# First four quads of a block attention with MLP: fused mask and maximum, value sums off TensorE, one transfer per quad, and a new order

## The chip, the cores and the metric

One core of one Trainium2 chip runs the whole kernel. The metric is the device time of the program in microseconds (us); of each kernel the median of several runs is taken. A profile of one execution gives, beside it, the time of every instruction on the core's engines: TensorE (PE, with its weight loads PEld), VectorE (DVE), ScalarE (ACT), GpSimd (POOL), and SyncE (SP), which here issues nearly all transfers. "Span" is the time from the first to the last instruction of that execution. KB are 1,024 bytes.

## The reference

Attention of 4 sequences of 768 tokens, 8 heads of 64, in which a token sees the tokens within 15 places, and beside them 24 summaries of its whole sequence: one per block of 32 tokens, the maximum of the keys and the mean of the values. Its result goes through an MLP.

```python
k_sum = k.reshape(B, H, nb, block, D).max(axis=3)       # block = 32, nb = 24
v_sum = v.reshape(B, H, nb, block, D).mean(axis=3)
scores_l = scale * np.matmul(q, k.transpose(0, 1, 3, 2))
scores_s = scale * np.einsum('bhsd,bhnd->bhsn', q, k_sum) + np.log(block)
scores_l_m = np.where(abs(pos[:, None] - pos[None, :]) < 16, scores_l, -1e9)
a = softmax(np.concatenate([scores_l_m, scores_s], axis=-1))
attn = np.matmul(a, np.concatenate([v, v_sum], axis=2))
...
h = x @ w_in                                            # (3072, 512) @ (512, 2048)
g = h * erf(softplus(h))
out = g @ w_out                                         # (3072, 2048) @ (2048, 512)
```

## The kernel before

The 3,072 tokens are six chunks of 512, the 8 heads four pairs; a chunk and a pair make a **quad**, of which there are 24. A quad has eight blocks of 64 queries, each against a window of 96 keys and 24 summaries: 120 columns (`NK`, with `LW` = 96). The MLP runs in 24 periods, four per chunk, each for 512 of the 2,048 inner columns: `mm1` makes h (line L836), `hout`, `soft`, `erfs` and `gsplit` make g, `mm2` adds g times w_out into four output banks (L1006 and L1010; from the ninth period on h is made from seven products instead, L879, L882 and L888). Quads are made ahead of the period that needs them.

The first four quads open the program, and nothing of the MLP can run before them. For each quad p:

- `load_qk_first` brings its keys (384 KB, L510) and queries (256 KB, L511); `load_vw_first` brings its windows of values (512 KB, L518). The values as such, from which the means come, are two transfers of 768 KB for all four quads (`load_v_first`, L515), tokens on partitions.
- `ksum_first` takes the 24 block maxima of the keys on VectorE (L521).
- `scores`: TensorE writes a mask into two PSUM banks (`mask`: per bank a bf16 matmul of an identity with `mask_h`, L588, and one that adds log 32, L589), then adds the products of queries with keys and with the summaries (L597).
- `softmax`: VectorE takes the maximum of each block (`red`: two reductions, L636, and a scaling, L638); ScalarE takes the exponential from PSUM with its sum (L644); VectorE makes reciprocals (L648, L649) and normalises (L654), or ScalarE does (L657).
- `vsum_first`: six matmuls with a selecting matrix `pick` (L527) add the values of 32 tokens each, for all four quads in one bank; ScalarE copies the bank (L531), and for each quad its 24 rows are repeated into the window tile `vwf`: on ScalarE three times and by a DMA once (L535).
- `transp` (L684, copied by ScalarE, L689), `av` (the product with the values, L729) and `xsplit` (high part of x on ScalarE, low part on VectorE, L748) give the input of `mm1`.

The weights come as sixteen raw tiles of 1 MB (`load_w`, L334), the first two w_in tiles first. `convert` makes a float32 tile of each on VectorE (L354, L357, L360, about 128x1024 elements each), and `split` a high part on ScalarE and a low part on VectorE (L376). A matmul of h needs both parts of x and both of w. From quad 4 on masks are not made on TensorE: `add` is one VectorE instruction for each block (L630) that adds the mask to the scores, writes the result, and gives the negative maximum; `MQ` = 4 is the quad from which this holds.

The order of all work is made when the program is built: `Plan` records each step with its engines, a cost for each, and what it reads and writes; `order` walks through time by these costs, takes on each engine the ready step with the smallest key, and lets a step that may run on two engines go to the one that ends first. `TUNE` shifts keys, and pins some steps to an engine. While TensorE has a gap in that plan, `busy` puts in matmuls on zeros (L1058) that write a bank named `idle`, until the first step that needs that bank. Each engine then executes its list in order, waiting at each instruction for what it needs. SP's transfers take eight semaphores in turn, so that a transfer is issued only when the eighth before it has landed.

## Time and profile before

| what | before |
|---|---|
| time, median of 3 runs | 600.77 us (600.4 to 601.37) |
| span of the profiled execution | 599.2 us |
| TensorE busy | 591.9 us, 99% of the span |
| VectorE busy | 476.3 us, 79% |
| ScalarE busy | 425.4 us, 71% |
| GpSimd busy | 4.0 us, 1% |
| read from and written to memory | 135.66 and 31.46 MB |

Busy time is the union of an engine's instructions. Matmuls overlap each other, and a busy TensorE may be at filler work. An engine's busy share says little by itself where stages differ, so the rows below are read by stretches of time: the opening up to the first matmul of h, and the rest. The chain of waits is followed from the last instruction back to what released each step; one that starts with SP's issue and a transfer means that the transfer queue was the limit there.

### The profile page before, as it was taken

How to read it: one execution, taken by the hardware profiler on the slowest of the kernel's cores; microseconds unless marked ns; L12 is line 12 of the kernel's file. 1: busy time of each engine (PE TensorE's matmuls, PEld its weight loads, DVE VectorE, ACT ScalarE, POOL GpSimd, SP SyncE). 2: the span in 40 equal slices, each digit the busy share in tenths (PEclk: the TensorE clock that was granted, in tenths of full speed). 3: DMA queues.
4: the chain of work that ended last, by engine and by line, in shares of the span. 5: the costliest groups of instructions: out<-in, count | busy, mean ns of one | idle time of the engine just before them, and what ended most of it. 6: DMA issues, size and time to landing. Idle time of an engine off the chain costs nothing.

```text
span 599.2 us, 11732 instructions
## 1 busy us (share of the span) xinstructions
PE 591.9 (99%) x4515; PEld 486.9 (81%) x4515; DVE 476.3 (79%) x1001; ACT 425.4 (71%) x827; POOL 4.0 (1%) x30
## 2 busy tenths in 40 slices
PE   8999999999999999999999999999999999999997
PEld 4675666878888889889888888888888888888885
DVE  5999999888999987867989769669778677656552
ACT  6989889989979894674886964746646654852571
POOL 2000000000000000000000000000000000000000
PEclk9999999999999999999999999999999999999999
DMA  8999768578987989899898889777798863764622
GB/s 313 350 412 357 288 232 308 205 258 293 314 349 244 363 310 336 307 357 363 311 366 315 321 315 326 284 278 284 261 320 275 298 236 141 259 236 175 244 71 71
DMA packets 47955, 169.94 MB, mean 284 GB/s; under 512 B 4444, under 2 KB 17692, under 8 KB 35356
## 3 DMA queue, kind: packets, MB, share of 16 engines
q1 hardware_dynamic: 47324, 168.67, 77.7%
q8 instruction: 35, 0.57, 0.4%
q10 hardware_dynamic: 576, 0.52, 0.3%
q14 instruction: 20, 0.16, 0.1%
HBM read 135.66 MB, written 31.46 MB: 279 GB/s over the span
## 4 chain that ended last, share of the span: by engine, by line
PE 95%; DMA 2%; DVE 1%; SPq 1%; issue 0%; ACT 0%; DVEq 0%
PE ops L1010 41%; PE h L836 15%; PE ha L888 11%; PE hb L882 7%; PE ops L1006 5%; PE hb L888 4%; PE hb L879 4%; PE pA L597 3%; PE px L732 3%; DMA rw<-w_in 2%; PE px L729 1%; PE pA L684 1%; PE pB L597 0%; SPq L515 0%; SPq L511 0%; SPq L510 0%
## 5 line engine op out<-in xcount | busy, mean ns | idle before, releaser
L1010 PE MATMUL ops<-w,gh 128*128 128x512 f32 x704 | 230.2, 393 | 0.0
L1010 PEld LDWEIGHTS ops<-w,gh 128*128 128x128 f32 x704 | 132.3, 188 | 27.7 <-issue 0.9
L1010 PE MATMUL ops<-w,gl 128*128 128x512 f32 x352 | 137.5, 391 | 0.0
L1272 ACT ACT_TABLE_LOAD x98 | 125.7, 1283 | 1.7
L836 PE MATMUL h<-x,w 128*128 128x512 f32 x384 | 97.1, 402 | 0.0
L298 ACT COPY hc<-hb 128x256 f32<-128x256 f32 x65 | 23.9, 373 | 102.0 <-PE hb L879 55.9
L836 PEld LDWEIGHTS h<-x,w 128*128 128x128 f32 x384 | 71.1, 188 | 18.5 <-issue 3.7
L1010 PEld LDWEIGHTS ops<-w,gl 128*128 128x128 f32 x352 | 66.2, 188 | 11.8
L986 DVE TENSOR_TENSOR hc<-wt,hc 128x1024 f32<-128x1024 f32 x44 | 53.0, 1219 | 10.7 <-ACT wt L974 10.7
L644 ACT ACTIVATE prx<-prx,stats 128x120 f32<-128x120 f32 x160 | 61.0, 384 | 0.2
L993 DVE TENSOR_TENSOR gl<-hc,gh 128x1024 fp32r<-128x1024 f32 x44 | 53.6, 1220 | 1.0 <-ACT gh L298 0.2
L927 DVE TENSOR_TENSOR hc<-hb,hc 128x256 f32<-128x256 f32 x96 | 38.7, 418 | 15.8 <-ACT hc L298 14.8
L974 ACT ACTIVATE wt<-wt 128x1024 f32<-128x1024 f32 x48 | 50.1, 1059 | 0.4
L962 ACT ACTIVATE wt<-hc 128x1024 f32<-128x1024 f32 x32 | 33.0, 1056 | 8.2 <-DVE hc L927 8.0
L298 DVE CAST gh<-hc 128x1024 fp32r<-128x1024 f32 x37 | 25.5, 690 | 10.6 <-PE ops L1010 9.5
L882 PE MATMUL hb<-w,ws 128*128 128x512 f32 x96 | 30.2, 396 | 0.0
L644 ACT ACTIVATION_READ_ACCUMULATOR prx<-prx,stats 128x1 f32 x160 | 30.0, 188 | 0.0
L1006 PE MATMUL ops<-a32s,gw 128*128 128x512 f32 x64 | 29.6, 597 | 0.0
L630 DVE CUSTOM_DVE_ANT_0 prx<-pA,mask_sb 128x120 f32<-128x120 f32 x64 | 14.2, 278 | 17.7 <-PE pB L597 17.5
L298 DVE COPY hc<-hb 128x256 f32<-128x256 f32 x31 | 13.0, 418 | 18.0 <-PE hb L879 13.9
L888 PE MATMUL ha<-w,ws 128*128 128x256 f32 x192 | 27.2, 283 | 0.0
L888 PE MATMUL ha<-x,w 128*128 128x256 f32 x192 | 27.2, 282 | 0.0
(173 smaller groups left out, 961.8 us busy)
## 6 DMA issues: line engine op xcount, KB each, us to landing
w<-dr SPq DMA_DIRECT2D x36, 1024.0 KB
ws<-ds SPq DMA_DIRECT2D x30, 1024.0 KB
vw<-v_win SPq DMA_DIRECT2D x20, 512.0 KB
kw<-k_win SPq DMA_DIRECT2D x20, 480.0 KB
rw<-w_in SPq DMA_DIRECT2D x8, 1024.0 KB
rw<-w_out SPq DMA_DIRECT2D x8, 1024.0 KB
dr<-w SPq DMA_DIRECT2D x8, 1024.0 KB
dt<-ot SPq DMA_DIRECT2D x16, 512.0 KB
```

The costliest lines, as they stand in the source:

```text
L298: e.copy(o, i) if e is nc.scalar else e.tensor_copy(o, i)
L644: nc.scalar.activation(s["pr"][:, j], s["pr"][:, j] if qd >= MQ else s["sc"][j // NI][:, i * NK:(i + 1) * NK], AF.Exp, scale=-1.0 if qd >= ...
L836: nc.tensor.matmul(hs[k, f][:, 0:T], lhsT=w[m], rhs=xt[ch, cc][:, x], start=(cc == 0 and n == 0), stop=(cc == 3 and n == 2))
L882: nc.tensor.matmul(full, lhsT=w[0], rhs=y, start=first and c == 0, stop=c == 1, skip_group_check=True)
L888: nc.tensor.matmul(half, lhsT=w[m], rhs=y[:, l], start=first and c == 0 and i == 0, stop=c == 1 and i == 2, skip_group_check=True)
L927: on({"DVE": 0.43}, lambda e: e.tensor_tensor(hc[k, n][:, m, z], bank(n, "b")[:, R], hc[k, n][:, m, z], op=ALU.add), [pair_banks(n)[1]], [ ...
L974: act(0.96, lambda n=n: nc.scalar.activation(wt[k, n], wt[k, n], AF.Erf, scale=-1.0 if k < SOFT else 1.0), [s], [s], table=("sig",), after ...
L986: e.tensor_tensor(hc[k, n], wt.pop((k, n)), hc[k, n], op=ALU.mult)
L993: e.tensor_tensor(gs[k, n][1], hc.pop((k, n)), f32(gs[k, n][0]), op=ALU.subtract)
L1006: nc.tensor.matmul(os_[ch, t], lhsT=x[0][:, i % 2, t * 128:(t + 1) * 128], rhs=w32["o", g, i // 2][:, i % 2], start=first, stop=last)
L1010: nc.tensor.matmul(os_[ch, t], lhsT=x[y][:, i % 2, t * 128:(t + 1) * 128], rhs=w[m], start=first and n == 0, stop=last and n == 2)
L1272: nc.scalar.preload_act_table_set(sets[o["load"]])
```

## The change

For the first four quads the mask leaves TensorE. `scores` starts each bank with the product itself, and `softmax` uses `add` for every quad, so that VectorE reads the scores from PSUM, adds the mask, and takes the maximum; ScalarE then reads the masked scores from SBUF. The masks become three rows (`masks`) picked by `mask_of`. The values of a quad are loaded by a transfer of their own (`vn`, 384 KB, heads on partitions as the keys are), and `vsum_first` adds them per quad: `add_groups`, one VectorE reduction or, on GpSimd, five additions that halve each group of 32; a matmul of 24 rows (L509 in the new file) with a scaled identity turns the sum; a small copy on VectorE or ScalarE takes it out, and the rows are repeated on VectorE, ScalarE or GpSimd. The idle bank is o2 now, the sums' bank o3, and the quads' score banks are other ones. Table and names of unused code go. `TUNE` is another table, 20 KB of numbers before and after, so the order of the whole program is new.

```diff
-TUNE = {3: (-38.72167, 1.5, 0, None), 4: (-0.388519, 1.5, 0, None), ...
+TUNE = {2: (-0.005207729, 1.5, 0, None), 3: (-0.04361445, 1.5, 0, None), ...
...
+    masks = sb([128, 3, NK], F32, "masks")
+    band, low_edge, high_edge = (masks[:, i] for i in range(3))
...
+    def mask_of(qd, j):
+        i = edge_at.get(mask_at[qd // NP % 3] + j % NI, 0)
+        return masks_q[:, i] if qd >= DT else masks[:, i]
...
+    part = sb([128, 128], F32, "part")
+    nc.scalar.mul(part, ident, 1.0 / 32.0)
...
-        first_dma(2.7 if p == 1 else 0.97, lambda: nc.sync.dma_start(out=kfirst[p], in_=k_nat[0, p]), w=[f"kf{p}"])
-        first_dma(0.66, lambda: nc.sync.dma_start(out=qfs[:, p], in_=q_t[0, p]), w=[f"qf{p}"])
-
-    def load_v_first():
-        for n in range(2):
-            first_dma(2.1 + 0.15 * n, lambda n=n: nc.sync.dma_start(out=vts[n], in_=v_tok[3 * n:3 * n + 3].rearrange("t s c -> s t c")), w=[f"vt{n}"])
+        first_dma(0.93, lambda: nc.sync.dma_start(out=kfirst[p], in_=k_nat[0, p]), w=[f"kf{p}"])
+        first_dma(0.62, lambda: nc.sync.dma_start(out=qfs[:, p], in_=q_t[0, p]), w=[f"qf{p}"])
+
+    def load_v_first(p):
+        first_dma((2.6, 1.8)[p] if p < 2 else 0.93, lambda: nc.sync.dma_start(out=vns[p // 2][:, p % 2], in_=v_nat[0, p]), w=[f"vn{p}"])
...
-    def vsum_first(bank):
-        def go(t):
-            if t == 0:
+    def add_groups(e, out, x):
+        if e is not nc.gpsimd:
+            return e.tensor_reduce(out, groups(x), op=ALU.add, axis=AX.X)
+        x, n = groups(x), 16
+        t = sb([128, NS, 16], F32, "halves", "ot")
+        while n:
+            o = t[:, :, 0:n] if n > 1 else out.unsqueeze(2)
+            e.tensor_tensor(o, x[:, :, 0:n], x[:, :, n:2 * n], op=ALU.add)
+            x, n = t, n // 2
+
+    def vsum_first(p, bank):
+        def go():
+            if p == 0:
                 tiles[bank] = ps("vs", bank)
-            nc.tensor.matmul(tiles[bank][0:NK], lhsT=pick[:, 20 - 4 * t:140 - 4 * t], rhs=vts[t // 3][:, t % 3], start=(t == 0), stop=(t == 5))
-        for t in range(6):
-            pe(0.87, lambda t=t: go(t), [f"vt{t // 3}"], [bank])
-        def summed():
-            nc.scalar.copy(vsum[LW:NK], tiles[bank][LW:NK].rearrange("s (p c) -> s p c", p=NP))
-        act(0.5, summed, [bank], [f"vsum0{p}" for p in range(NP)])
-        def rows_(e, p):
-            o, i = st[p]["vw"][LW:NK], vsum[LW:NK, p:p + 1, :].to_broadcast([NS, NB, 128])
-            e.dma_start(out=o, in_=i) if e is nc.sync else copy(e, o, i)
-        for p in range(NP):
-            on({"ACT": 0.95, "SP": 0.45} if p else {"DVE": 1.13, "ACT": 0.95}, lambda e, p=p: rows_(e, p), [f"vsum0{p}", f"vwf{p}"], [f"vwg{p}"])
+            nc.tensor.matmul(tiles[bank][LW:NK, 128 * p:128 * p + 128], lhsT=vs_sum[:, p, 0:NS], rhs=part, start=True, stop=True, skip_group_check=True)
+
+        def rows_(e):
+            copy(e, st[p]["vw"][LW:NK], vsum[LW:NK, p:p + 1, :].to_broadcast([NS, NB, 128]))
+
+        def summed(e):
+            copy(e, vsum[LW:NK, p], tiles[bank][LW:NK, 128 * p:128 * p + 128])
+        on({"DVE": 0.86, "POOL": 2.0}, lambda e: add_groups(e, vs_sum[:, p, 0:NS], vns[p // 2][:, p % 2]), [f"vn{p}"], [f"vs{p}", "ot"])
+        pe(0.25, go, [f"vs{p}"], [bank], small=1)
+        on({"DVE": 0.2, "ACT": 0.25}, summed, [bank], [f"vsum0{p}"])
+        on({"DVE": 1.13, "ACT": 0.95, "POOL": 1.6}, rows_, [f"vsum0{p}", f"vwf{p}"], [f"vwg{p}"])
...
-            for sc in s["sc"] if qd < MQ else []:
-
-                nc.tensor.matmul(sc[:, 0:NI * NK], lhsT=ident_h, rhs=mask_h[:, m0:m0 + NI], start=True, stop=False, skip_group_check=True)
-                nc.tensor.matmul(sc[:, 0:NI * NK].rearrange("q (i c) -> q i c", i=NI)[:, :, LW:NK], lhsT=ones, rhs=cst.rearrange("o (i c) -> o i c", i=NI), start=False, stop=False, skip_group_check=True)
...
-        def add(e):
-            t = s["pr"] = turned_keys if qd >= DT else prx[:, :, 0:NK]
+        def add(e, js=range(NB)):
+            t = s["pr"] = turned_keys if qd >= DT else prx[:, :, 0:NK] if qd >= NP else prs[qd // 2][:, qd % 2]
             s["mx"] = stat(0, par)
-            for j in range(NB):
+            for j in js:
                 i = j % NI
-                e.tensor_tensor_reduce(out=t[:, j], in0=four(s["sc"][j // NI][:, i * NK:(i + 1) * NK]), in1=four(mk[:, i]), scale=-0.125, scalar=3e38, op0=ALU.add, op1=ALU.min, accum_out=s["mx"][:, j:j + 1])
-
-        def red(e, halves=(0, 1)):
-            s["mx"] = stat(0, par)
-            s["pr"] = prs[qd // 2][:, qd % 2] if qd < NP else prx[:, :, 0:NK]
-            for a in halves:
-                e.tensor_reduce(s["mx"][:, NI * a:NI * a + NI], s["sc"][a][:, 0:NI * NK].rearrange("q (i c) -> q i c", i=NI), op=ALU.max, axis=AX.X)
-            m = s["mx"][:, NI * halves[0]:NI * halves[-1] + NI]
-            e.tensor_scalar(m, m, -0.125, None, op0=ALU.mult)
+                e.tensor_tensor_reduce(out=t[:, j], in0=four(s["sc"][j // NI][:, i * NK:(i + 1) * NK]), in1=mask_of(qd, j), scale=-0.125, scalar=3e38, op0=ALU.add, op1=ALU.min, accum_out=s["mx"][:, j:j + 1])
...
-    banks = [PA, ("h0", "h1"), ("o0", "o1"), ("h0", "h1")]
-    idle = ps("idle", "o3")
+    banks = [PA, ("h0", "h1"), PA, PA]
+    idle = ps("idle", "o2")
...
+        if p == 0:
+            convert(units[0])
+        vsum_first(p, "o3")
```

VectorE at the conversion of the first w_in tile, before (`a_348` is that tile's float32 form; `h_312` is a score bank of quad 3):

```order
L654 TENSOR_TENSOR prf<-prf,stats 128x960
L354 TENSOR_SCALAR a_348<-rw 128x1024
L357 SCALAR_TENSOR_TENSOR a_348<-rw,a_348 128x1024
L521 TENSOR_REDUCE ksum<-kf 128x24
L360 SCALAR_TENSOR_TENSOR a_348<-rw,a_348 128x1024
L648 TENSOR_SCALAR stats<-stats 128x8
L649 RECIPROCAL stats<-stats 128x8
L636 TENSOR_REDUCE stats<-h_312 128x4
L636 TENSOR_REDUCE stats<-h_313 128x4
L638 TENSOR_SCALAR stats<-stats 128x8
L376 TENSOR_TENSOR w<-a_348,w 128x1024
L654 TENSOR_TENSOR prf<-prf,stats 128x960
```

and now (`a_399` is that tile's float32 form; L327, L330, L333 and L349 are what L354, L357, L360 and L376 were, L623 what L654 was, L713 what L748 was):

```order
L271 COPY vsum<-vs 24x128
L327 TENSOR_SCALAR a_399<-rw 128x1024
L617 TENSOR_SCALAR stats<-stats 128x8
L618 RECIPROCAL stats<-stats 128x8
L330 SCALAR_TENSOR_TENSOR a_399<-rw,a_399 128x1024
L623 TENSOR_TENSOR prf<-prf,stats 128x960
L333 SCALAR_TENSOR_TENSOR a_399<-rw,a_399 128x1024
L271 CAST x<-px 128x512
L617 TENSOR_SCALAR stats<-stats 128x8
L618 RECIPROCAL stats<-stats 128x8
L713 TENSOR_TENSOR x<-px,x 128x512
L349 TENSOR_TENSOR w<-a_399,w 128x1024
```

The key maxima and the score maxima of quad 3 (L521, L636, L638) are no longer inside the conversion but ahead of it; two more pairs of reciprocals and the high part of x stand inside it.

SP's transfers up to the first w_in tile (`rw`), before:

```order
L511 DMA qf<-q_t 128x512
L510 DMA kf<-k_nat 128x768
L511 DMA qf<-q_t 128x512
L510 DMA kf<-k_nat 128x768
L515 DMA vt<-v_tok 128x3x512
L510 DMA kf<-k_nat 128x768
L511 DMA qf<-q_t 128x512
L515 DMA vt<-v_tok 128x3x512
L334 DMA rw<-w_in 128x2048
```

and now:

```order
L483 DMA kf<-k_nat 128x768
L484 DMA qf<-q_t 128x512
L483 DMA kf<-k_nat 128x768
L484 DMA qf<-q_t 128x512
L483 DMA kf<-k_nat 128x768
L484 DMA qf<-q_t 128x512 x2
L487 DMA vn<-v_nat 128x768
L483 DMA kf<-k_nat 128x768
L487 DMA vn<-v_nat 128x768
L490 DMA vwf<-v_win 128x1024
L307 DMA rw<-w_in 128x2048
```

The keys and queries of all quads but one key tile go first, then values quad by quad; ahead of the first `rw` stand a `kf`, a `qf` and a `vwf` more, and two `vn` of half the size of a `vt` instead of two `vt`.

TensorE at the first rows of h, where a `transp` ends and an `av` (`px`) stands, before:

```order
L684 MATMUL pA<-ident,prf 120x64
L684 MATMUL pB<-ident,prf 120x64
L729 MATMUL px<-ptr,vwf 64x64 x16
L836 MATMUL h<-x,w 128x512 x15
L729 MATMUL px<-ptr,vwf 64x64 x16
L836 MATMUL h<-x,w 128x512 x6
```

and now:

```order
L649 MATMUL pA<-ident,prf 120x64
L649 MATMUL pB<-ident,prf 120x64
L694 MATMUL px<-ptr,vwf 64x64 x16
L509 MATMUL vs<-part,vs_sum 24x128
L801 MATMUL h<-x,w 128x512 x12
L694 MATMUL px<-ptr,vwf 64x64 x16
```

The fourth quad's sum (`vs`) is now the last row ahead of h.

GpSimd held only constants and masks before; its last rows now are these (`halves` is the partial sum of a quad, `vn` its values):

```order
L271 COPY vwf<-vsum 24x1024
L502 TENSOR_TENSOR halves<-vn 128x384
L502 TENSOR_TENSOR halves<-halves 128x24x8
L502 TENSOR_TENSOR halves<-halves 128x24x4
L502 TENSOR_TENSOR halves<-halves 128x24x2
L502 TENSOR_TENSOR vs_sum<-halves 128x24
L271 COPY vwf<-vsum 24x1024
```

Ahead of them stand the sums of quads 0 and 1, a row copy and the sum of quad 2.

## Rows read from the trace of the kernel before

**Rows 1.** Page, part 1: busy time, share of span, instructions per engine.
```profile
PE 591.9 (99%) x4515; PEld 486.9 (81%) x4515; DVE 476.3 (79%) x1001; ACT 425.4 (71%) x827; POOL 4.0 (1%) x30
```

**Rows 2.** Windows: stretch, its length, busy us per engine, granted clock, DMA share, GB/s.
```profile
0.00:27.28 27.28, 23.80 (x428) 14.35 (x428) 20.10 (x36) 21.25 (x73) 3.99 (x30) 1.00 0.88 332
27.28:100.00 72.72, 72.72 (x495) 48.22 (x492) 72.34 (x128) 64.78 (x132) 0.00 (x0) 1.00 0.87 324
100.00:590.00 490.00, 490.00 (x3575) 420.18 (x3574) 382.59 (x836) 337.72 (x622) 0.00 (x0) 1.00 0.77 278
595.40:597.70 2.30, 0.00 (x0) 0.00 (x0) 0.42 (x1) 0.37 (x1) 0.00 (x0) 1.00 0.68 223
597.70:599.20 1.50, 0.00 (x0) 0.00 (x0) 0.00 (x0) 0.00 (x0) 0.00 (x0) 0.51 0.02 8
```

**Rows 3.** Waits of TensorE: waited for, us in total, times, longest (first of six).
```profile
PE idle L1058 <- DVE zeros L217: 1.1, 1, 1.1
```

**Rows 4.** Chain that ended last, 0 to 30 us: start, us, what.
```profile
5.64 11.52 DMA rw<-w_in
...
17.26 0.70 DVE a L354
...
17.99 1.23 DVE a L357
19.21 0.86 DVE ksum L521
20.08 1.13 DVE a L360
...
21.53 1.21 DVE stats L636 x2
...
22.94 1.21 DVE w L376
24.14 1.08 DVE prf L654
```

**Rows 5.** Timeline of VectorE: start, us, instruction, [idle before it, and releaser].
```profile
4.38 0.95 DVE L521 TENSOR_REDUCE ksum<-kf 128x24 f32<-128x768 f32 x1 [3.24 <-DMA kf<-k_nat]
...
25.13 0.68 DVE L748 TENSOR_TENSOR x<-px,x 128x512 fp32r<-128x512 f32 x1
...
49.03 0.28 DVE L630 CUSTOM_DVE_ANT_0 prx<-pA,mask_n 128x120 f32<-128x120 f32 x1
...
50.65 0.69 DVE L354 TENSOR_SCALAR a<-rw 128x1024 uint32<-128x1024 uint32 x1
```

**Rows 6.** Timeline of TensorE, parts of 0 to 40 us.
```profile
1.06 3.03 PE L1058 MATMUL idle<-zeros 128*128 128x512 bf16 x7 [1.06 <-DVE zeros L217]
...
9.98 1.95 PE L527 MATMUL vs<-vt,pick 128*120 128x512 f32 x4 [0.22 <-DMA vt<-v_tok]
...
16.04 0.37 PE L588 MATMUL h<-mask_h,small 128*128 128x480 bf16 x1
...
22.95 1.68 PE L1058 MATMUL idle<-zeros 128*128 128x512 bf16 x7
...
39.05 0.39 PE L1058 MATMUL idle<-zeros 128*128 128x512 bf16 x1
```

**Rows 7.** Timeline of GpSimd, 0 to 7 us.
```profile
1.01 0.29 POOL masks.py:199 TENSOR_SCALAR_AFFINE_SELECT ident<-ident 128x128 f32<-128x128 f32 x1
...
1.50 0.26 POOL L232 TENSOR_SCALAR_AFFINE_SELECT band<-band 64x96 f32<-64x96 f32 x1
```

**Rows 8.** Timeline of SP: issue of the third w_in load.
```profile
14.61 0.33 SPq L334 DMA_DIRECT2D rw<-w_in  x1
```

**Rows 9.** DMA, 0 to 35 us in 40 slices: GB/s moved.
```profile
GB/s 0 0 239 380 334 236 186 321 343 376 420 398 419 431 424 410 410 392 403 415 403 412 426 417 403 431 403 431 300 66 92 207 281 431 403 403 403 459 449 421
```

**Rows 10.** Chain that ended last, 205 to 216 us: blocks of twelve h matmuls.
```profile
208.10 2.72 PE h L836 x12
...
211.50 1.08 PE px L732 x32
212.58 2.94 PE h L836 x12
```

124 lines of the change are left out of this document (36 added, 88 removed).

## Prediction

> **What bounds the kernel now.** I read the page's busy lines first: TensorE is busy for 591.9 of 599.2 us, VectorE for 79%, ScalarE for 71%, GpSimd for 1% [rows 1]. A kernel like this gets shorter only where TensorE waits, or where TensorE has less to do. The windows say where it waits: in the first 27.28 us it is busy 23.80 us, and from there to 590 us it is busy in every stretch for the whole stretch [rows 2]. The list of waits agrees: it has six waits in all, 1.1 us and less, the last before 25.4 us [rows 3]. So the time is: the moment at which the first L836 matmul (the h product) starts, plus 572 us of TensorE work that never waits. What sets that moment is in the chain [rows 4]: the queue of transfers up to the first w_in tile (issued at 5.64, landed 11.52 us later), then VectorE without a pause: converting that tile (L354, L357, L360, L376) with a ksum and two maxima between and a normalising multiply behind, until 25.2; then TensorE's transposes and output product for the next quad, and h at 27.3. TensorE is "busy" before that, but with masks, value sums and idle fillers that nobody is waiting for at the end. The profiled execution spans 599.2 us and the three runs have a median of 600.77, so 1.6 us lie around the span; I take differences from the trace and subtract them from 600.77.
>
> **The change, part by part.**
>
> *Masks off TensorE.* Sixteen matmuls (L588, L589) go. The last pair lies at 16 us, ahead of the w_in tile's landing [rows 4, 6], so what they took on TensorE is worth nothing at the end. VectorE pays: per quad two reductions (1.21 us [rows 4]) and a small scaling become eight fused instructions with their eight accumulator reads. Those exist already for later quads: eight take from 49.03 to 50.65, 1.62 us [rows 5]. That is 0.2 to 0.4 us more per quad, and in the new order all of it stands before the first conversion.
>
> *Value sums.* Six L527 matmuls (two of them 1.95 us [rows 6]) go, again off the chain. In their place stand four sums on GpSimd (five instructions each), four 24-row matmuls, four small copies, and three of the four row copies on GpSimd instead of ScalarE and a DMA. GpSimd is busy for 4 us in the kernel before, all of it in the opening [rows 2], so the room is there; the price is not in the trace. Bounds: from below the VectorE reduction of as much data, 0.95 us; from GpSimd's own rows, 0.26 us for 96 columns and 0.29 for 128 [rows 7], so about 1 ns a column and 0.16 us an instruction, plus 0.06 between two: 744 columns in five instructions come to 1.85 us, and to 2.6 if a second operand doubles the columns. I take 2.2, between GpSimd's two values, and 1.2 for a row copy of 1,024 columns.
>
> *First transfers.* They land in order of issue. In KB queued: 640 at 4.38, 2,048 at 9.9, 3,456 at 14.6 (when the third w_in load, which stands eight places behind that transfer, goes out) and 4,480 at 17.2 [rows 4 to 6, 8]. In the new order the first w_in tile ends at 4,864 KB: a k, a q and a vwf tile more stand ahead (1,152 KB), and the v tiles are half the size (768 KB less). At the last rate (1,024 KB in 2.55 us) that is 0.95 us later, **18.1**. The DMA that waited in SP's queue for the vsum copy is gone; behind it the transfers sank to 66 GB/s [rows 9]. But SP's later loads only refill: up to the fourth w_in tile both orders carry about the same KB, so I cost that at nothing.
>
> *VectorE, from the first transfer to the first h.* In the new order it does ksum 0, ksum 1, the four fused maxima, ksum 2 and 3, two pairs of reciprocals and two normalisings *before* the first conversion. ksum 1 needs 1,024 KB: 5.9 us on the old curve, 5.3 if its slow stretch (186 GB/s at 6 us [rows 9]) falls elsewhere. From the end of ksum 1 at 6.9: 4 x 1.62 + 2 x 0.86 + 2 x 0.32 + 2 x 1.08 + two small copies of 0.2, 11.4 us, so VectorE reaches the conversion at 18.3, just behind the tile. Then L327 0.73, a reciprocal pair 0.32, L330 1.23, normalising 1.08, L333 1.13, the high part of x 0.68 at most, a reciprocal pair 0.32, its low part 0.68, the low part of w 1.21 [rows 4, 5]: 7.4 us, and 0.14 to TensorE: **h starts at 25.8 instead of 27.3**. The ksum and two maxima that stood inside that stretch (0.86 + 1.21) pay for the later landing. TensorE's other work ahead of h (two more transposes, one output product, one sum) is due earlier: the fourth vn tile ends at 6,144 KB, 21.3 us; GpSimd's sum for quad 3 ends near 24.7 and its matmul at 25. Gain **1.5 us**; 2.5 if the tile lands where it did, 0.8 if ksum 1 and the transposes come later by some tenths each.
>
> *The order made anew.* The same matmuls follow the first h. Between large tiles and a run of small ones (scores, transposes, output products) TensorE loses time: twelve h matmuls take 2.72 us, and 2.94 right behind an output product [rows 10]. Counting the rows of the two orders from the first h on, TensorE makes 32 such visits before and 31 after, 4 and 3 lone L485 transposes, and one idle filler (0.24 us, [rows 6]) is gone: 0.22 for the visit, as much for the transposes, 0.24, **0.7 us**, between 0.5 and 1.0. Whether a wait returns behind 27 us can't be read from an order. VectorE and ScalarE are nearly full until 100 us [rows 2], so a TensorE that comes 1.5 us sooner needs them sooner; VectorE's order gives that up to the first gw product (it has left a ksum, a maximum and one load's first step behind it), and ScalarE has 17 table loads fewer over the kernel (82 rows for 99), so I cost new waits at nothing and keep them in the range.
>
> Sum: 600.77 - 1.5 - 0.7 = **598.6**.
>
> **The rivals.**
>
> *1. GpSimd's sums come late.* TensorE takes its instructions in order, and the matmul for quad 3's sum now stands just ahead of the first h. Vn 2 lands at 19.1; then two sums and one row copy on GpSimd, and 0.5 us to TensorE. With 2.2 and 1.2 that is 25.2, harmless. With 3.2 us a sum and 1.3 a copy it is 27.3, and the start gains nothing: 600.1. Against it: 3.2 is above both values from rows.
>
> *2. TensorE's clock falls.* The idle fillers stop in the new order before the first output product, because the bank they write (o2) is the one that product takes; in the kernel before they go on to 39 us. From the second value sum (16.8) to the first output product (18.5, behind the row copy on GpSimd) TensorE stands still, and it is idle for half of 17 to 26 us. In this trace the granted clock was 1.00 (2.4 GHz) while TensorE stood idle from 595.4, and was 0.51 (1.2 GHz) in the stretch from 597.7 [rows 2]. A fall costs what the start shows: seven fillers in 3.03 us against 1.68 later [rows 6], 1.35 us: 600.0.
>
> *3. GpSimd and VectorE shut each other out: the slower side.* Nothing in this trace has both at work on SBUF at once behind the first memsets, so no row shows or excludes it. In the 7.4 us of the conversion VectorE has four instructions with two SBUF operands (1.23 + 1.08 + 1.13 + 1.21) and L327 (0.73), 5.4 us, and GpSimd has two sums and a row copy, 5.6 us. If these can't overlap, they need 11.0 us instead of 7.4; h starts at 29.4, 2.1 us after the old start, or 30.6 with another row copy in it: 1.4 to 2.6 us above 600.77 after the 0.7 from the order, in the middle **602.8**. It turns slower once GpSimd holds VectorE back by 2.2 us. The Trainium skill has this as a rule (SBUF — State Buffer, "SBUF: two separate sides"): VectorE and GpSimd share one pair of ports as an exclusive lock, against GpSimd instructions that read SBUF also where VectorE has two SBUF inputs. By that rule rival 3 would come true in part at least; no run here shows it. Against it speaks that VectorE's single-operand work (2 us) leaves gaps, and that GpSimd's short instructions (0.2 us each) hold little: whoever waits, waits for one instruction.
>
> **How the numbers follow.** About 0.2%, 1.2 us, is what can be told from no change. Forecast 598.6 (597.2 to 599.5): 0.56. Rival 1, 600.1: 0.16. Rival 2, 600.0: 0.11. Rival 3, 602.8: 0.17, most of it above 602. Faster 0.56, same 0.27, slower 0.17. The low end, 596.9, is the start at 24.8 (2.5 us) and 1.0 us from the order, with a little for work I have not seen; the high end, 602.5, takes in half of rival 3.
>
> **What would show it.** Right: no L588 and L527 rows, first h between 25 and 26.5, no TensorE wait behind it, fewer than 592 us busy. L327 should start at 18 to 18.7 with either the w_in transfer or VectorE itself ahead of it. Rival 1: the L509 matmul before h waits for a GpSimd L502 row of over 3 us a quad. Rival 2: granted clock 0.5 between 17 and 30 us and h matmuls at twice 0.227 us. Rival 3: L330, L333, L349 longer than 1.22 us or idle in front of them while GpSimd works, or L502 rows several times their column price. Wrong altogether: waits of TensorE on VectorE or ScalarE between 40 and 130 us, which this order would then have made.

## The result and the profile after

| | before | after |
|---|---|---|
| time, median | 600.86 us (600.40 to 601.37) | 608.02 us (607.44 to 608.18) |
| ratio | | 1.0114 (95% interval 1.0100 to 1.0129) |
| span of the profiled execution | 599.2 us | 606.1 us |
| first h matmul | 27.28 us | 31.94 us |
| from there to the end of the span | 571.9 us | 574.2 us |

The change made the kernel 7.2 us slower; 598.6 was forecast, with a range to 602.5. Of the 6.9 us of span, 4.7 are lost before the first h matmul (L801 now) and 2.2 right behind it.

The page's busy line after, which answers [rows 1]:

```profile
PE 592.8 (98%) x4499; PEld 489.5 (81%) x4499; DVE 474.0 (78%) x1038; ACT 405.6 (67%) x823; POOL 21.9 (4%) x38
```

GpSimd went from 4.0 to 21.9 us, and ScalarE from 425.4 to 405.6, which is the 17 table loads of 1.28 us that the prediction counted; TensorE and VectorE hardly moved. The windows, as in [rows 2] (stretch, its length, busy us of PE, PEld, DVE, ACT, POOL, granted clock, DMA share, GB/s), tell more:

```profile
0.00:31.94 31.94, 22.61 (x414) 15.28 (x414) 26.23 (x93) 22.21 (x85) 21.38 (x38) 0.87 0.96 380
31.94:37.43 5.49, 5.49 (x15) 3.88 (x16) 4.54 (x4) 2.35 (x3) 0.49 (x1) 0.50 1.03 415
37.43:100.00 62.57, 62.41 (x400) 41.52 (x401) 59.26 (x98) 48.27 (x84) 0.00 (x0) 1.00 0.68 248
100.00:590.00 490.00, 490.00 (x3623) 418.98 (x3622) 379.56 (x839) 330.30 (x648) 0.00 (x0) 1.00 0.79 283
```

All of GpSimd's new work lies ahead of h. The first twelve h matmuls ran at a granted clock of 0.50 and took 5.49 us; twelve take 3.0 at full clock (from 39.10 us in the same trace). Behind 37.43 us nothing more is lost: those 2.5 us cover the 2.2. The waits of TensorE (waited for, us in total, times, longest), against one of 1.1 us and five shorter before [rows 3]:

```profile
PE vs L509 <- POOL vs_sum L502: 5.7, 2, 3.6
PE px L694 <- POOL vwf L271: 1.6, 2, 1.2
```

And the chain that ended last, which in the kernel before ran through the w_in transfer and VectorE [rows 4], runs through GpSimd (start, us, what):

```profile
18.86 1.81 POOL halves L502
...
23.42 1.01 POOL vs_sum L502
24.50 1.93 POOL vwf L271
26.50 1.01 POOL halves L502
27.58 1.46 POOL halves L502
...
31.12 0.23 POOL vs_sum L502
31.39 0.62 PE vs L509 x2
```

Quad 3's sum ends at 31.35, its small matmul stands ahead of h in TensorE's order, and h starts when that is done. VectorE had the low part of w ready at 28.5. That TensorE's clock was low can be read one step earlier (windows of 1 us, the last of 0.5, same columns):

```profile
21.00:22.00 1.00, 0.00 (x0) 0.00 (x0) 0.97 (x4) 1.00 (x6) 0.92 (x2) 1.00 1.09 442
...
23.00:24.00 1.00, 0.00 (x0) 0.00 (x0) 1.00 (x2) 0.15 (x1) 0.92 (x2) 0.92 0.94 389
24.00:25.00 1.00, 0.51 (x2) 0.16 (x2) 1.00 (x2) 0.00 (x0) 0.94 (x2) 0.50 1.02 414
...
37.50:38.00 0.50, 0.50 (x20) 0.50 (x22) 0.00 (x0) 0.00 (x0) 0.00 (x0) 1.00 1.10 459
```

TensorE did nothing from 20.9 to 24.5 us, waiting for quad 2's sum; within that pause the clock fell from 2.4 to 1.2 GHz, and it came back when TensorE had run h without a gap from 31.9 to 37.4.

Last, GpSimd and VectorE beside each other. GpSimd's timeline (start, us, instruction):

```profile
10.18 1.02 POOL L502 TENSOR_TENSOR halves<-vn 128x384 f32<-128x384 f32 x1 [6.47 <-DMA vn<-v_nat]
11.28 1.40 POOL L502 TENSOR_TENSOR halves<-halves 128x192 f32<-128x192 f32 x3
...
18.86 1.80 POOL L502 TENSOR_TENSOR halves<-vn 128x384 f32<-128x384 f32 x1
20.75 2.59 POOL L502 TENSOR_TENSOR halves<-halves 128x192 f32<-128x192 f32 x3
23.42 1.02 POOL L502 TENSOR_TENSOR vs_sum<-halves 128x24 f32<-128x24 f32 x1
```

and VectorE's:

```profile
14.52 1.15 DVE L623 TENSOR_TENSOR prf<-prf,stats 128x960 f32<-128x960 f32 x1
...
18.09 1.71 DVE L623 TENSOR_TENSOR prf<-prf,stats 128x960 f32<-128x960 f32 x1
...
20.16 1.06 DVE L327 TENSOR_SCALAR a<-rw 128x1024 uint32<-128x1024 uint32 x1
...
27.15 1.43 DVE L349 TENSOR_TENSOR w<-a,w 128x1024 fp32r<-128x1024 f32 x1
```

The sum of quad 0, made while VectorE only added masks to scores that it read from PSUM (L608), took 2.8 us from its first to its last row (10.18 to 12.99); the sums of quads 1, 2 and 3 took 3.6, 5.6 and 4.8. L327 is 1.06 us long where L354 was 0.70 [rows 4], the L623 at 18.09 takes 1.71 where the one at 14.52 took 1.15. So three things stand in this trace at once: a late sum, a fallen clock, and two engines that lengthen each other. The experiments take them apart.

### The profile page after: what moved, and what is told of

It is laid out like the page before. It is cut to its first block, busy times and chain, and to the rows that moved or that the text cites. A ratio compares the mean times of both kernels' runs of the same rounds, so it can differ in the third digit from the quotient of the medians.

```text
span 606.1 us, 11769 instructions
## 1 busy us (share of the span) xinstructions
PE 592.8 (98%) x4499; PEld 489.5 (81%) x4499; DVE 474.0 (78%) x1038; ACT 405.6 (67%) x823; POOL 21.9 (4%) x38
## 4 chain that ended last, share of the span: by engine, by line
PE 93%; ACT 2%; POOL 2%; DVE 1%; DMA 1%; issue 0%; SPq 0%; POOLq 0%
PE ops L966 40%; PE h L801 14%; PE ha L850 11%; PE hb L844 7%; PE hb L850 4%; PE hb L841 4%; PE ops L962 3%; PE pA L574 3%; PE px L697 3%; POOL halves L502 1%; PE px L694 1%; ACT L1225 1%; DMA qf<-q_t 1%; PE pB L574 1%; DVE prf L608 1%; ACT prx L613 1%
## 5 line engine op out<-in xcount | busy, mean ns | idle before, releaser
L966 PE MATMUL ops<-w,gh 128*128 128x512 f32 x704 | 227.4, 393 | 0.0
L966 PEld LDWEIGHTS ops<-w,gh 128*128 128x128 f32 x704 | 132.2, 188 | 28.5 <-issue 1.3
L801 PE MATMUL h<-x,w 128*128 128x512 f32 x384 | 97.5, 407 | 0.0
L801 PEld LDWEIGHTS h<-x,w 128*128 128x128 f32 x384 | 72.7, 192 | 19.6 <-issue 2.6
L889 DVE TENSOR_TENSOR hc<-hb,hc 128x256 f32<-128x256 f32 x96 | 39.1, 418 | 22.1 <-ACT hc L271 21.6
L924 ACT ACTIVATE wt<-hc 128x1024 f32<-128x1024 f32 x32 | 32.4, 1052 | 19.4 <-DVE hc L889 17.1
L271 DVE CAST gh<-hc 128x1024 fp32r<-128x1024 f32 x34 | 23.5, 690 | 7.8 <-PE ops L966 7.2
L850 PE MATMUL ha<-x,ws 128*128 128x256 f32 x192 | 26.7, 282 | 0.0
L850 PEld LDWEIGHTS ha<-x,w 128*128 128x128 f32 x192 | 24.8, 190 | 0.2
```

The source lines that it names most:

```text
L271: e.copy(o, i) if e is nc.scalar else e.tensor_copy(o, i)
L801: nc.tensor.matmul(hs[k, f][:, 0:T], lhsT=w[m], rhs=xt[ch, cc][:, x], start=(cc == 0 and n == 0), stop=(cc == 3 and n == 2))
L850: nc.tensor.matmul(half, lhsT=w[m], rhs=y[:, l], start=first and c == 0 and i == 0, stop=c == 1 and i == 2, skip_group_check=True)
L889: on({"DVE": 0.43}, lambda e: e.tensor_tensor(hc[k, n][:, m, z], bank(n, "b")[:, R], hc[k, n][:, m, z], op=ALU.add), [pair_banks(n)[1]], [ ...
L966: nc.tensor.matmul(os_[ch, t], lhsT=x[y][:, i % 2, t * 128:(t + 1) * 128], rhs=w[m], start=first and n == 0, stop=last and n == 2)
```

## The experiments

Each was timed beside the kernel before (600.9 to 601.3 us in these rounds), and ratios are against it. "Changed kernel" is the kernel after.

**The late sum.** The small matmul of quad 3 is moved behind the first twelve h matmuls in the finished order:

```diff
+    late = next(o for o in plan if o["r"] == ["vs3"])
+    plan.remove(late)
+    plan.insert(next(i for i, o in enumerate(plan) if o["r"] == ["w0", "xh0", "xl0"] and o["w"] == ["o1"]) + 1, late)
```

> The changed kernel, in which the matmul that turns quad 3's value sum stands behind the first twelve h matmuls instead of ahead of them; nothing else is moved. Theory A (the first h waits for GpSimd's sum of quad 3): h starts when VectorE has the low part of w, at about 28.7 us instead of 31.9, with the clock still at 0.50; TensorE then has the other half of the h block to give at 1.2 GHz as before; time 608.0 - 3.2 = 604.8 us. Rival (the late sum only stands in front of something else that is equally late, the row copy into the windows of quad 3 or the second conversion): h starts at 28.7, the same time is lost at the next output products, 607 to 608 us.

Measured: 605.72 us, ratio 1.0080 (1.0063 to 1.0097), 2.3 less than the changed kernel.

```profile
27.98 1.97 PE L694 MATMUL px<-ptr,vwf 120*64 120x64 f32 x32 [1.20 <-POOL vwf L271]
29.89 4.68 PE L801 MATMUL h<-x,w 128*128 128x512 f32 x12
```

h comes at 29.89, in an execution in which everything up to there was 0.65 us later than in the first (quad 3's sum starts at 27.14 instead of 26.50); so the start moved by 2.7 us. Theory A had 3.2; the rest is quad 1's output product, which takes 1.97 us at 1.2 GHz and now sets the start. From h to the end of the span it is 573.6 us (574.2 in the changed kernel), so the rival's losses further on don't appear.

**The clock.** Idle matmuls are put into the three pauses, on a bank that is free:

```diff
-    idle = ps("idle", "o2")
+    idle = ps("idle", "o0")
...
+            busy({"vs2": 14, "vwg1": 4, "vs3": 8}.get(o["r"][-1], 0))
```

> The changed kernel, with the idle matmuls on a bank that is free until the first h (o0), and 14, 4 and 8 of them in TensorE's three long pauses at 20.9, 26.2 and 29.3 us. Theory B (the granted clock fell because TensorE stood still from 20.9 us): the clock stays at 1.00, h starts at 31.7 (GpSimd's sum sets it, not TensorE), the first twelve h matmuls take 2.7 to 2.9 us instead of 5.49; time 608.0 - 2.6 - 0.2 = 605.2 us. Rival (the clock falls for another reason, such as all engines and transfers at work at once): the clock is 0.50 from 24 us all the same, 608 us or more.

Measured: 605.50 us, ratio 1.0074 (1.0059 to 1.0089). The windows of that run:

```profile
24.00:28.00 4.00, 2.77 (x49) 1.80 (x51) 3.94 (x7) 2.53 (x7) 3.78 (x4) 1.00 1.00 410
...
31.60:34.60 3.00, 3.00 (x15) 2.23 (x15) 2.96 (x3) 1.40 (x3) 0.72 (x1) 1.00 1.01 399
```

The clock holds, h starts at 31.60, and behind it the span has 571.7 us, 0.2 less than before. So the clock cost 2.5 us, theory B. Whether the new order as such gives anything can't be told from this: the 0.2 is one execution. Of the runs below that keep the clock in the h block and move nothing behind its start, four have 571.9 to 572.2 us there and a fifth 573.1; three executions in the old order have 571.9 to 572.0.

**Both.** Both edits, without the idle matmuls ahead of quad 3's sum.

> The two edits together: quad 3's sum matmul behind the first twelve h matmuls, and 14 and 4 idle matmuls in the pauses at 20.9 and 26.2 us. If the late sum and the clock are two separate losses, their gains add: h at 28.7 us with the clock at 1.00 and 2.8 us for the first twelve h matmuls, 608.0 - 3.2 - 2.8 = 602.0 us. What is left above the forecast of 598.6 is then VectorE's later conversion (28.7 instead of 25.8). If they overlap (the clock would have come back anyway), 604 us.

Measured: 603.81 us, ratio 1.0053 (1.0034 to 1.0073): 4.2 of the 6.0 us that were expected of the two. h starts at 29.36, 0.7 of that because the experiment's own four idle matmuls hold up quad 1's output product (VectorE had let its bank go at 27.6). The gains nearly add. What is left is 2.7 us above the kernel before: 2.1 in the start of h and 0.6 behind it, where quad 3's small matmul (0.4 us) now stands. The start is late by those idle matmuls and by VectorE: from L327 at 19.45 to the instruction behind L349 at 28.89 the conversion takes 9.4 us, where 7.4 were forecast.

**GpSimd off the job.** The sums go to VectorE, the row copies to ScalarE, at the same places of the order:

```diff
+    for o in plan:
+        if o["on"] == "POOL":
+            o["on"] = "DVE" if o["r"][0][:2] == "vn" else "ACT"
```

> The changed kernel, with GpSimd out of the opening: its four value sums are VectorE reductions, its three row copies ScalarE copies, each at the same place of the order. Theory C (GpSimd and VectorE hold each other up): VectorE gets 4 x 0.95 = 3.8 us of work more but its other instructions are back at their lengths of the kernel before (L623 1.08, L327 0.70, L330 and L349 1.22; they were about 1.8 us longer in all), so the low part of w ends near 30.5 instead of 28.5, no TensorE wait on GpSimd is left, and h starts at 30.7 at a clock of 0.50: 606.8 us. Rival (GpSimd is merely slow and VectorE loses nothing by it): VectorE's instructions keep their lengths, h starts at 32.4 or later, 608.5 us.

Measured: 606.81 us, ratio 1.0090 (1.0073 to 1.0107). VectorE's instructions are back at their lengths:

```profile
26.28 1.15 DVE L623 TENSOR_TENSOR prf<-prf,stats 128x960 f32<-128x960 f32 x1
27.35 1.22 DVE L333 SCALAR_TENSOR_TENSOR a<-rw,a 128x1024 uint32<-128x1024 uint32 x1
...
30.93 1.22 DVE L349 TENSOR_TENSOR w<-a,w 128x1024 fp32r<-128x1024 f32 x1
```

That is theory C's sign, but h came at 33.5, not 30.7, so its sum was wrong: VectorE has no 3.8 us to give here, and TensorE's clock fell twice, behind a wait of 1.7 us for quad 1's queries at 6 us and again from 28 to 34 us, where h stands. The time fits theory C, the path does not; the run shows the lengths and no more.

**Contention by itself.** The kernel before, untouched but for GpSimd instructions that nobody waits for:

```diff
+    load_a = sb([128, NS, 32], F32, "load_a", "ot")
+    load_b = sb([128, NS, 16], F32, "load_b")
+    nc.gpsimd.memset(load_a, 0.0)
+    for _ in range(15):
+        nc.gpsimd.tensor_tensor(load_b, load_a[:, :, 0:16], load_a[:, :, 16:32], op=ALU.add)
```

> The kernel before, with 15 additions on GpSimd (128x384 from SBUF to SBUF, the form of the first step of a value sum) that nobody waits for, from about 4.5 us on; nothing else is changed. It measures contention alone. If GpSimd is the side that pays: its additions take 1.0 us while VectorE stands still or reads PSUM and 1.8 us or more beside VectorE instructions with two SBUF operands, VectorE's L357, L360, L376 and L654 are 0.0 to 0.3 us longer, h starts 0.5 to 1 us later, 601.4 to 601.9 us. If the two exclude each other fully and VectorE pays as much (rival 3 of the prediction): h starts 3 us later, 604 us.

Measured: 606.47 us, ratio 1.0089 (1.0074 to 1.0104). Fifteen additions that nobody uses cost 5.4 us, most of it contention, as the rows show. GpSimd's row and some of VectorE's (L643 is the small scaling that was L638, L526 the key maximum, L653 the first of the pair of reciprocals, L359 and L362 the first two steps of the conversion):

```profile
7.87 19.89 POOL L283 TENSOR_TENSOR load_b<-load_a 128x384 f32<-128x384 f32 x15
```

```profile
7.88 1.03 DVE L643 TENSOR_SCALAR stats<-stats 128x4 f32<-128x4 f32 x1
...
17.57 0.81 DVE L643 TENSOR_SCALAR stats<-stats 128x8 f32<-128x8 f32 x1
...
20.38 1.49 DVE L359 TENSOR_SCALAR a<-rw 128x1024 uint32<-128x1024 uint32 x1
21.90 1.92 DVE L362 SCALAR_TENSOR_TENSOR a<-rw,a 128x1024 uint32<-128x1024 uint32 x1
23.74 0.94 DVE L526 TENSOR_REDUCE ksum<-kf 128x24 f32<-128x768 f32 x1
...
25.74 0.97 DVE L653 TENSOR_SCALAR stats<-stats 128x8 f32<-128x8 f32 x1
```

An instruction of 0.17 us (L643, L653) takes up to 1.03: it waits for the addition that GpSimd is at. The L643 of 17.57 ends at 18.38, and the addition beside it ran from 17.35 to 18.35. L359 and L362 get 0.8 and 0.7 us longer in the same way; the reductions (L526) keep their 0.94. The additions come every 1.33 us in place of 1.1. So the first expectation (VectorE loses little) falls, and rival 3 of the prediction has the mechanism right: the low part of w starts at 28.14 us, against 22.94 [rows 4]. The Trainium skill states it (SBUF — State Buffer, "SBUF: two separate sides"), for a VectorE instruction in a mode that takes both port pairs, or with two SBUF inputs against a GpSimd instruction that reads SBUF: whichever of the two starts first "gets the pair for the whole instruction; the other fully blocks". This trace agrees, with 0.86 us on a 0.17 us instruction.

The run isn't contention alone, though. TensorE waited 1.7 us for the key maximum of quad 3, and the clock fell here too (a window, and TensorE's idle matmuls, which take 1.68 us in the kernel before [rows 6]):

```profile
28.00:31.00 3.00, 3.00 (x13) 0.95 (x9) 2.97 (x6) 2.67 (x10) 0.00 (x0) 0.50 0.92 384
```

```profile
28.19 3.17 PE L1063 MATMUL idle<-zeros 128*128 128x512 bf16 x7
```

h comes 5.7 us later (32.98 us). VectorE is done with the multiplication that TensorE needs next at 30.43 instead of 25.21, which is 5.2 us of it; the rest, about 0.5 us, is an estimate for the idle matmuls at half clock, behind which TensorE went on only at 31.29. So contention led to a pause and a lower clock without any late sum.

**Shorter GpSimd instructions.** The same with copies of 128x384, first 15, then 32:

```diff
-        nc.gpsimd.tensor_tensor(load_b, load_a[:, :, 0:16], load_a[:, :, 16:32], op=ALU.add)
+        nc.gpsimd.tensor_copy(load_b, load_a[:, :, 0:16])
```

> The same with 15 one-operand copies (128x384, SBUF to SBUF) in place of the additions. If what is contended for is SBUF access as such: copies are stretched beside VectorE as the row copies in the changed kernel were (1.04 to 1.92 us), and VectorE loses as much as by the additions: 601.4 to 601.9 us. If a second operand is what matters: copies keep their length, VectorE too, 600.9 us.

Measured: 601.44 us, ratio 1.0008 (0.9999 to 1.0018). It decides nothing: the 15 copies came every 0.62 us and were over at 17.1 us, before the conversion began. Hence the longer stream:

> The kernel before with 32 one-operand GpSimd copies that nobody waits for, 0.62 us each, so that they last from 7.8 us until about 28 us; the 15 of the earlier run had ended at 17.1, before the first conversion. The additions (15, until 27.8) cost 5.4 us. If every GpSimd instruction that reads and writes SBUF holds VectorE up for the rest of its own length: about the same number of VectorE instructions wait, each for half as long, some 3 us, 604 us. If two operands are needed on GpSimd's side: VectorE's instructions keep their lengths in the conversion, 601.4 us as with 15 copies.

Measured: 603.91 us, ratio 1.0040 (1.0025 to 1.0055), 2.65 us.

```profile
7.84 26.93 POOL L283 COPY load_b<-load_a 128x384 f32<-128x384 f32 x32
```

```profile
17.51 0.99 DVE L359 TENSOR_SCALAR a<-rw 128x1024 uint32<-128x1024 uint32 x1
18.54 1.40 DVE L362 SCALAR_TENSOR_TENSOR a<-rw,a 128x1024 uint32<-128x1024 uint32 x1
```

L359 is 0.3 us longer and L362 0.2, where additions made it 0.8 and 0.7, and no instruction of 0.17 us takes more than 0.47; a copy by itself takes 0.51. The mean clock is 1.00 here, so the 2.65 us are contention alone. One operand on GpSimd's side is enough, and for these two lengths VectorE pays at most about the length of one GpSimd instruction each time.

**The sums back on TensorE.** The six matmuls of the kernel before, in the changed kernel's opening, GpSimd with the row copies only.

In the finished order (`find(r, w)` is the step that reads r and writes w; `behind(a, b)` in this run puts a behind b):

```diff
+        loads_, sums_, mms_, outs_ = find((), [f"vn{p}"]), find([f"vn{p}"], [f"vs{p}", "ot"]), find([f"vs{p}"], ["o3"]), find(["o3"], [f"vsum0{p}"])
+        sums_["fn"] = lambda e: None
+        for o, fn in ((loads_, load_vt), (mms_, sum_vt)):
+            o["fn"] = (lambda e, fn=fn, p=p: fn(p)) if p < 2 else lambda e: None
...
+    behind(find((), ["vwf0"]), find((), ["w0"]))
+    behind(find(["vsum00", "vwf0"], ["vwg0"]), find(["o3"], ["vsum01"]))
```

> The changed kernel with the fused masks, the new order and the early key and query loads kept, and only the value sums given back to TensorE: two transfers of 768 KB in place of the four of 384 KB (the first w_in tile then ends at 5,120 KB instead of 4,864), six matmuls, one ScalarE copy; GpSimd keeps three row copies and nothing else; idle matmuls on the bank o0 until the first output products. If the forecast failed at the GpSimd sums and the clock alone: VectorE reaches the conversion at 18.5 us, its instructions have the lengths of the kernel before, h starts at 26.1 us with the clock at 1.00; with the gain of the new order as the other runs show it (0.2 instead of 0.7) 600.9 - 1.2 - 0.2 = 599.5 us. Rival (VectorE's list before the conversion, not GpSimd, is what is too long): h starts at 27.5 or later, 601 us or more.

Measured: 605.44 us, ratio 1.0076 (1.0059 to 1.0093). VectorE reached the conversion at 19.0 us with all lengths restored, in an execution whose second key tile landed 0.8 us later than in the changed kernel's; but the sums (5.7 us of TensorE) stood behind quad 3's scores, quad 0's output product came at 26.0, and VectorE sat idle for 3.9 us waiting for it. So the placing was at fault, and a second run put the sums earlier:

Here and in the next run `behind(a, b, ...)` is turned round, and puts b and what follows it behind a; "fill" is a number of idle matmuls ahead of a step:

```diff
+    behind(find((), ["w0"]), find((), ["vwf0"]))
+    behind(find(["qf2", "ksum02"], ("pA", "pB")), find(["vs0"], ["o3"]))
+    behind(find(["sm2"], ["rs2"]), find(["o3"], ["vsum01"]), find(["vsum00", "vwf0"], ["vwg0"]), find(["pt", "vwf0", "vwg0"], ["o2"]))
```

> The sums on TensorE again, as in the earlier run, but placed so that they are early: three of the six matmuls ahead of quad 3's scores, three behind quad 0's transposes, the one copy of the result on VectorE inside the conversion, GpSimd with three row copies only, idle matmuls in the pauses. In the earlier run VectorE's list was at the conversion at 19.0 us with transfers 0.8 us late and its instructions had their old lengths; the output product for quad 0 came at 26.0 because the sums stood behind quad 3's scores. If that placing was the whole loss: output product for quad 0 at 22.5, h at 26.5, 601.0 - 0.7 - 0.2 = 600.1 us. If fused masks and early key loads are no gain even so: h at 27.3 or later, 601 us or more.

Measured: 607.01 us, ratio 1.0097 (1.0077 to 1.0117). No better, even in the one of its four executions that kept the clock (605.63 us; the others had mean clocks of 0.993 to 0.995): VectorE waited 1.2 us for the sums, and then the row copies fell into the conversion:

```profile
24.74 1.99 DVE L627 TENSOR_TENSOR prf<-prf,stats 128x960 f32<-128x960 f32 x1
26.66 2.06 DVE L337 SCALAR_TENSOR_TENSOR a<-rw,a 128x1024 uint32<-128x1024 uint32 x1
```

Both are 0.8 us too long. The kernel before had these copies on ScalarE and a DMA. Since both runs stumble over their own placing, they don't show what the sums on GpSimd cost.

**Half the sums out of the way.** Quads 2 and 3 summed on VectorE behind the first conversion.

```diff
...
+        o = find([f"vn{p}"], [f"vs{p}", "ot"])
+        o["on"] = "DVE"
...
+    behind(find(["gl0", "w0"], ["w0"]), find(["vn2"], ["vs2", "ot"]))
+    behind(conv1[2], find(["vn3"], ["vs3", "ot"]))
```

> The changed kernel with the value sums of quads 2 and 3 as VectorE reductions behind the first w_in conversion instead of on GpSimd inside it; quads 0 and 1 stay on GpSimd; their matmuls, copies and quad 2's output product stand later in the order accordingly, idle matmuls on o0 fill the pauses. If contention inside the conversion is the cause: L330, L333, L349 back at 1.2 us, h at 27.0 us, clock 1.00, and TensorE waits for no sum: 600.5 us. If VectorE has no room behind the conversion either: TensorE waits at quad 2's output product for up to 2 us, 602.5 us.

Measured: 607.68 us, ratio 1.0089 (1.0060 to 1.0118). L330, L333 and L349 are back at 1.2 as expected, but TensorE paused for 2.0 us for its next output product, the clock fell at 27 us, and the gain was lost; the one execution whose mean clock was 1.000 took 604.21, still 3.0 us above the kernel before, which no trace explains.

**Nothing on GpSimd at all.** Is the rest of the forecast sound? First the sums alone are left out:

```diff
+    for p in range(NP):
+        find([f"vn{p}"], [f"vs{p}", "ot"])["fn"] = lambda e: None
+    find(["pr2"], ("pA", "pB"))["fill"] = 10
+    find(["w0", "xh0", "xl0"], ["h1"])["fill"] = 6
```

> The changed kernel without the four value sums on GpSimd (they are left out, so the mean rows of the first four quads are zero; their transfers, their matmuls, copies and the three row copies on GpSimd stay), with idle matmuls on o0 that keep TensorE going. It shows what is left of the forecast when no sum is late, no sum contends and the clock stays: VectorE at the conversion at 19.5 us (20.16 less the 0.63 us by which L623 was longer), 7.4 us of conversion, h at 27.0 us, clock 1.00: 601.0 - 0.3 - 0.2 = 600.5 us. If only the sums stood between the forecast and the result: h at 25.8, 599.3 us. If the row copies on GpSimd contend as the sums do: L330, L623 and L333 still 0.2 to 0.6 us longer, h at 28 us, 601.5 us.

Measured: 605.33 us, ratio 1.0056 (1.0035 to 1.0077), with executions from 602.66 (mean clock 1.000) to 606.23 (0.994). The profiled one, at 605.66, lost its clock early:

```profile
6.00:8.00 2.00, 0.03 (x1) 0.00 (x0) 1.53 (x8) 0.35 (x2) 0.00 (x0) 0.85 1.02 384
8.00:10.00 2.00, 1.81 (x54) 1.84 (x57) 1.99 (x13) 2.00 (x13) 0.00 (x0) 0.50 1.04 414
```

TensorE waited 2.2 us there for quad 1's queries. The kernel before has masks to write in such places: those of quads 0 and 2 from 3.93 to 4.83 us, that of quad 1 from 6.88 to 7.55. The row copies that were left on GpSimd still stretched VectorE: L349 took 2.02 us. Then sums and row copies are left out and the clock is held:

```diff
+    for p in range(NP):
+        find([f"vn{p}"], [f"vs{p}", "ot"])["fn"] = lambda e: None
+        o = find([f"vsum0{p}", f"vwf{p}"], [f"vwg{p}"])
+        if o["on"] == "POOL":
+            o["fn"] = lambda e: None
+    find(["qf1", "kf1"], ("h0", "h1"))["fill"] = 4
+    find(["pr2"], ("pA", "pB"))["fill"] = 10
+    find(["w0", "xh0", "xl0"], ["h1"])["fill"] = 6
```

> The changed kernel with GpSimd idle in the opening: its four value sums and its three row copies are left out (the mean rows of quads 0 to 2 keep the zeros of their transfers, quad 3's are zero too); masks, transfers, the new order, the small matmuls and copies stay. Idle matmuls on o0 stand ahead of quad 1's scores (4), quad 2's transposes (10) and h (6), so that the clock holds. Without the sums alone the time was 602.7 in the one execution whose clock was 1.00, and a row copy on GpSimd still stretched L349 to 2.02 and L617 to 1.02 us. If GpSimd's hold on VectorE is all that stands against the forecast: VectorE at the conversion at 19.2 us, the low part of w 7.4 us later, h at 26.7, 600.0 us (1 us below the kernel before at most, so at the edge of what can be told). If the fused masks and the new order are themselves too long for VectorE: L327 at 20 us or later with nothing stretched, h at 28 us or later, 601.5 us or more.

Measured: 602.13 us, ratio 1.0023 (1.0014 to 1.0032). L327 came at 20.12 and nothing was stretched: the second expectation. But six idle matmuls of the experiment stood in front of h, so once more without them:

```diff
-    find(["w0", "xh0", "xl0"], ["h1"])["fill"] = 6
```

> The run before once more (GpSimd idle in the opening, sums and three row copies left out), without the six idle matmuls ahead of h, which had held h up there: quad 1's output product ended at 27.2 us, quad 3's small sum matmul at 27.5, and h came at 28.6. If that product (which waits for VectorE to take the low part of quad 0's x out of bank o2 at 26.0) and the small matmul are what now set the start: h at 27.5 with transfers as late as there, 27.0 with the earlier ones, 602.1 - 1.1 = 601.0 us, the kernel before within 0.2%. So the new opening would be worth nothing even with GpSimd's part for nothing. If h can follow the low part of w at once: 26.5 us, 600.0 us.

Measured: 601.91 us, ratio 1.0010 (1.0001 to 1.0020). This is what the change is worth with GpSimd's part for nothing and the clock held by idle matmuls: no gain. VectorE and TensorE ahead of h in this run:

```profile
20.67 0.70 DVE L327 TENSOR_SCALAR a<-rw 128x1024 uint32<-128x1024 uint32 x1
...
25.93 0.64 DVE L713 TENSOR_TENSOR x<-px,x 128x512 fp32r<-128x512 f32 x1
26.49 1.22 DVE L349 TENSOR_TENSOR w<-a,w 128x1024 fp32r<-128x1024 f32 x1
```

```profile
26.63 1.15 PE L694 MATMUL px<-ptr,vwf 120*64 120x64 f32 x32 [1.49 <-DVE x L713]
27.71 0.40 PE L509 MATMUL vs<-part,vs_sum 128*24 128x128 f32 x2
28.04 3.03 PE L801 MATMUL h<-x,w 128*128 128x512 f32 x12
```

All four output products use bank o2, so quad 1's can't start before VectorE has taken the low part of quad 0's x out of it (L713), and product and sum matmul stand ahead of h.

**Does an earlier h help at all?** The kernel before, with six h matmuls ahead of quad 1's output product, six more behind it, and quad 2's transposes and normalising later:

Here `behind(a, b)` puts a behind b again:

```diff
+    behind(find(["rs2"], ["pr2"]), find(["o2", "xh0"], ["xl0"]))
+    first = ["w0", "xh0", "xl0"]
+    for bank in ("o0", "o1"):
+        o = find(first, [bank])
+        plan.remove(o)
+        plan.insert(plan.index(find(["pt", "vwf1", "vwg1"], ["o2"])), o)
+    turn2 = find(["pr2"], ("pA", "pB"))
...
+    behind(turn2, find(first, ["h1"]))
+    behind(copy2, turn2)
```

> The kernel before with one change of order: the first six h matmuls stand ahead of quad 1's output product, six more behind it, quad 2's transposes behind these, and VectorE makes the low part of x ahead of quad 2's normalising. In the trace of the kernel before, h waits at 25.4 us for nothing but its place behind that product and those transposes. If the start of h is what counts: h at 25.4 instead of 27.3; 0.6 us of it are the transposes that now come later and 0.2 to 0.4 us two more changes between small and large tiles, so 600.9 - 1.0 = 599.9 us. Rival (the second quad's x is late instead, and TensorE waits for it behind the first twelve): 600.9 us or more.

Measured: 601.90 us, ratio 1.0014 (1.0005 to 1.0024).

```profile
24.76 1.43 PE L836 MATMUL h<-x,w 128*128 128x512 f32 x5 [0.22 <-DVE x L748]
...
39.13 4.63 PE L836 MATMUL h<-x,w 128*128 128x512 f32 x18
```

One h matmul starts at 24.03 us, the other five at 24.76, 2.5 us earlier than in the kernel before; 0.5 of that is this execution, in which the first w_in tile was taken up at 16.73 instead of 17.26. At 39.1 us, where the kernel before has its row at 39.09, as many h matmuls are done and nothing is left of it. The expectation forgot the output product itself (1.1 us), which moved behind with the transposes (0.6). The rest is small (the first 36 h matmuls stand in six stretches instead of four, and an output product takes 1.42 us instead of 1.15) and isn't taken apart. The start of h is a measure only as long as the same work stands ahead of it. In the changed kernel that holds: two output products and three quads' transposes, as before.

## Why the prediction was wrong

The frame was right: the time is the start of h plus 572 us. Taken by its steps, the forecast start of 25.8 became 31.94, and the rest came out 2.9 worse than forecast:

| step | forecast | measured | worse by |
|---|---|---|---|
| VectorE at the first conversion | 18.3 us | 20.16 us | 1.9 |
| conversion, L327 to the instruction behind L349 | 7.4 us | 8.34 us | 0.9 |
| from there to h | 0.14 us | 3.44 us | 3.3 |
| clock in the first h block | none | 2.5 us | 2.5 |
| gain of the new order (one execution) | 0.7 us | 0.2 us | 0.5 |
| sum | | | 9.1 of 9.4 |

- **Masks and first transfers: right.** Eight fused instructions took 1.6 us, and the first w_in tile was there at 17.3 (18.1 forecast; the transfer eight places behind it goes out at 17.29); VectorE, not the tile, was late.
- **VectorE up to the conversion: mis-sized.** In the changed kernel's trace the second key maximum ended at 6.77 us, where 6.9 was put, so the 1.9 us came behind it. VectorE waited 0.8 us for scores, where the sum had no wait; the L623 at 18.09 was 0.6 longer than the one before it; the small copies took 0.33 instead of 0.2; the rest is tenths. With GpSimd idle L327 still came at 20.1 to 20.7 us: no L623 was longer there, but the second key maximum ended only at 8.1 and 7.9. In the profiled executions it began at 5.8 to 7.1 us, since the tile lands at another moment each time, and 6.9 had been the densest packing of the transfers.
- **Conversion: right without GpSimd** (6.95 us from 20.67 to 27.62 in the last run with GpSimd idle), 0.9 short with it, and 2.0 short in the run of both edits. (Two pairs of reciprocals stand in it, one more than before, as the sum has it; the text on the change says two more.)
- **The value sums: the step that failed.** Bounds of 1.85 to 2.6 us were drawn from instructions of 96 and 128 columns that ran alone. The fastest sum takes 2.8, already outside; beside VectorE's conversion it takes up to 5.6. So quad 3's sum ended at 31.35 us, where 24.7 was put, and the 0.14 us from the low part of w to h became 3.44. An upper bound that holds no row in which the two engines meet is not one.
- **From the low part of w to h: failed too.** That TensorE's other work ahead of h "is due earlier" is not so: quad 1's product waits for bank o2. Even with GpSimd idle h starts 1.47 us behind the end of L713, for the product and the small matmul, and that is 0.4 behind L349, not 0.14.
- **The new order: at most 0.2, not 0.7.** The count of changes between tiles was taken as a gain; four other executions that keep the clock show none (571.9 to 572.2 us behind the start of h, 571.9 before).
- **The rivals** were named rightly, and all three came true, in one execution. Rival 1's sum ended at 31.35 us, rival 2's clock cost 2.5 us (1.35 was put down, from the fillers of the start), rival 3's contention was about 5 us with additions and 2.65 with copies, where it was measured in the kernel before. The chances had treated them as cases that exclude each other. They are a chain: VectorE and GpSimd hold each other up, so the sum is late, so TensorE stands still, so its clock falls, so h is slow. The argument against rival 3, that whoever waits waits for one instruction, was true and small comfort: several of VectorE's instructions waited, and GpSimd waited too. And its 0.2 us an instruction was the price of the small ones: the first addition of a sum takes 1.0.

Still open: no run separates the cost of the fused masks alone, or tells the sums on TensorE from a bad placing of them, and the runs show no version that beats the kernel before.
